# A table of steps in place of a list scheduler: attention block and gated MLP on one core

## The chip, the cores and the metric

The kernel runs on one core of a Trainium2 chip. The metric is the device time of one execution in microseconds (us). The engines are named as the profile names them: PE (TensorE, matrix products), DVE (VectorE), ACT (ScalarE), POOL (GpSimd) and SP (SyncE, which here only issues transfers). Each engine works through its own list of instructions. Transfers are carried by 16 DMA engines.

## The reference

A transformer block on 2048 tokens of width 512, in float32:

```python
qkv = (layernorm(x) @ wqkv).reshape(1, 2048, 3, 32, 16)      # 32 heads of 16
scores = einsum("bhqd,bhkd->bhqk", q, k) * 16 ** -0.5
scores = where((i - j >= 0) & (i - j < 256), scores, -1e9)   # a window of 256 keys
h = x + (softmax(scores) @ v) @ wo
n = layernorm(h)
out = h + (sigmoid(n @ w_gate) * (n @ w_up)) @ w_down         # hidden width 1376
```

## The kernel before

**Arithmetic.** float32 operands of the large products are split into a high and a low float16 part (`split`: `copy` makes the high part at L237 on ACT or L239 on DVE, `subtract` the low part at L244), and a product is three float16 products (`mm3`, L284: high x high, high x low, low x high). Weights get a power-of-two scale from their largest absolute value: `bound` (L249, L251) and `scale`, whose small product on PE is L262.

**Attention** goes by 8 blocks `b` of 256 tokens and, in a block, by 8 groups `g` of four heads. The pieces of work are generator functions. `do_ln` normalizes a tile of 128 tokens (statistics L417 on DVE, a power L423 on POOL, the scaling L432, the split) and turns it over on PE (L454) or by a DMA. `do_qk` makes queries and keys of a block, `do_v` the values (both in `mm3`), `do_keys` writes the keys to DRAM (L515) and loads them stacked three high into SK (L522), `do_queries` stacks the queries into SQ (L531). `do_s` computes the scores once for their row maxima: eight products (L585) into a ring of three PSUM banks, and after each one a row maximum on DVE (`row_max`, L570), which frees the bank. `do_m` turns the maxima into two extra rows of SQ. `do_st` computes the scores transposed with the maximum taken off (L639 to L650, a ring of two banks), ACT takes the exponentials (`exps`, L615), POOL masks them (`far` L623, `dia` L628). `do_pv` is the weighted sum over the values (L676, float32), its result goes to `rh` (high part L237, low part L688), is turned over by a DMA (L699, tile RT) and added on POOL (`do_o`, L706). `do_wo` divides by the softmax sum (L718, L720), splits (`whl`), turns over by a DMA (tile oT) and multiplies with `wo`.

**MLP.** The hidden width is cut into 512, 512 and 352 columns. The first four token tiles go one by one: `do_early` computes their first 512 columns while attention still runs, with PSUM copied to SQ on DVE (L830), and `do_gu` the rest. The other twelve go in pairs by a Strassen-like scheme, seven products in place of eight: `do_pair` prepares the sums of token halves, `do_T` the sums of weight quarters (load, split L904 and L906, four subtractions in the load's tile at L919, split again L923 on ACT and L926 on DVE), and `do_group` is one pair with one part of the hidden width: seven products of six matmuls each (L1027) in three PSUM banks, with evacuations and sums on ACT, DVE and POOL between them. `do_down` multiplies with `w_down` and stores.

**What sets the order.** The kernel is written for engines whose lists are fixed when it is built. Each generator yields, step by step, a cost for every engine that may do the step, the keys of what it needs, and the rings (PSUM banks, buffers) of which it takes a place. `Planner` runs a list scheduler over these: it keeps a clock for each engine, models the start of each ready step (`start`), and on each engine grants the ready step that starts first; among those within a small tolerance (`eps`) the one with the lowest priority number (`pick`). For a step that several engines may do it compares the modelled ends (`better`). All priorities, offsets and biases are numbers in one dictionary `C`, and `alt` leaves a step to one engine unless its name is in `C["alts"]`. PE's cost is stretched by a model of its clock (`stream`).

Of the kernel before, what the change touches and what calls it, by code (L numbers as in the profile page):

```python
# [36 lines left out]
T = 2048  # L37
# [21 lines left out]
C = dict(T=[148.182, 280.933], ln7=-7.501, s=5.429, pv=39.123, o=4.672, wo=[30.36, 31.212], v=[12.599, 24.978], qk=[-12.405, 3.564], ln=[-8.702, -6.351], m=-21.936, am=338.233, amd=118.201, sp=[287.055, -17.738], l2=[68.786, 20.751], ngu=4, gu=[64.904, 0.734], sd=[-171.116, 73.748], Tg=[16.516, 52.23], Tu=[-222.738, 17.484], Tb=[-146.461, -3.199], stash=155.192, l2b=-109.019, eps=0.064, prep=[-243.079, 245.157, 1.957, -60.084], alts=['hi', 'raw', 'whi', 'wsc', 'amax', 'pt', 'on', 'hhi', 'qk'], look=0.0, blog=413.973, bias={'ACT': -9.573, 'DVE': 7.071, 'POOL': -15.707}, pet=8, npv=2, down=6.634, lw=[-75.362, -59.481, -0.005, 74.029], lx=[-8.688, -47.634, 14.356, 9.926, 203.463, 96.796, 168.915], fill=[-71.831, 121.643, 130.507], clear=[-64.533, -23.452], write=-298.105, slack=167.929, stack=-112.133, off={'ln': [-166.66, -0.25, -4.616, -3.823, 11.91, 32.661, 62.31, 64.356], 'qk': [-171.929, -6.135, -32.431, 64.031, 63.96, -1.291, 0.767, 60.185], 'v': [188.33, 69.219, 54.263, -107.364, 206.961, 55.229, 34.243, 107.232], 's': [-163.512, -0.768, 31.21, 39.136, -344.985, -8.781, 4.748, 80.39], 'wo': [52.242, 40.433, 173.071, 59.896, 100.92, 72.757, 141.062, -184.237], 'o': [95.122, -281.215, 28.752, -120.215, 253.442, -30.242, -120.978, 95.302], 'pv': [-429.156, -31.744, 41.816, -12.207, -99.804, -46.682, 68.082, -169.17], 'm': [-74.099, -46.67, -98.34, -10.409, -56.92, 36.197, -114.381, -34.099]}, prep2=[89.331, -93.273, 2.384, 49.139], warm=[6.577, 9.585, 8.612, 11.534, 12.673, 21.472, 19.465, 25.332, 31.19])  # L59


LAG = {"PE": 0.2, "DVE": 0.2, "ACT": 0.19, "POOL": 0.1, "DMA": 0.0}
OWN = {"PE": 0.0, "DVE": 0.06, "ACT": 0.05, "POOL": 0.0, "DMA": 0.0}
TICK = 10.24 / 3
SWITCH = 0.095


class Planner:

# [7 lines left out]
    def __init__(self, rings):  # L77
        self.clock = dict.fromkeys(ENGINES, 0.0)
        self.clock[DMA_] = 0.65
        self.clock[POOL_] = 3.4  # L80
        self.moved = 0.0
        self.rings = rings
        self.freed = {r: [] for r in rings}
        self.done = {}
        self.parked = {}
        self.live = {e: [] for e in ENGINES}
        self.best = {}
        self.count = 0
        self.busy = {}
        self.on = None  # L90
        self.mode = 0

    def add(self, prio, piece, step=0.0):
        self.count += 1
        self.submit([prio, self.count, step, piece, next(piece), None])

    def submit(self, item):
        costs, needs = item[4][:2]
        for k in needs:
            if not isinstance(k[0], float) and k not in self.done:  # L100
                self.parked.setdefault(k, []).append(item)
                return
        times = [k if isinstance(k[0], float) else self.done[k] for k in needs]
        item[5] = {e: max([0.0] + [t + (OWN if f == e else LAG)[f] for t, f in times]) for e in costs}
        for e in costs:
            self.live[e].append(item)
            self.changed(e)

    def changed(self, eng):
        for e in (eng,) if eng in (PE_, DMA_) else (DVE_, ACT_, POOL_):  # L110
            self.best.pop(e, None)

    def mark(self, key, t):
        self.done[key] = t
        for item in self.parked.pop(key, ()):
            self.submit(item)

    def free(self, ring, n, t):
        self.freed[ring][n] = t
        self.best.clear()  # L120

    def start(self, eng, item):
        t = max(item[5][eng], self.clock[eng])
        rings = item[4][2] if len(item[4]) > 2 else ()
        for i, r in enumerate(rings):
            n = len(self.freed[r]) - self.rings[r] + rings[:i].count(r)
            if n >= 0:
                f = self.freed[r][n]
                if f is None:
                    return None  # L130
                t = max(t, f[0] + (OWN if f[1] == eng else LAG)[f[1]])
        return t

    def better(self, eng, t, item):

        costs = item[4][0]
        for e, cost in costs.items():
            if e != eng:
                first = sum(i[4][0][e] for i in self.live[e] if i[5][e] <= t + C["look"] and i[0] < item[0])
                if max(item[5][e], self.clock[e] + C["blog"] * first) + cost + C["bias"][e] < t + costs[eng] + C["bias"][eng]:  # L140
                    return True
        return False

    def pick(self, eng):
        if eng not in self.best:
            c = []
            for item in self.live[eng]:
                t = self.start(eng, item)
                if t is not None and not (len(item[4][0]) > 1 and self.better(eng, t, item)):
                    c.append((t, item[0], item[1], item))  # L150
            if c:
                t0 = min(c)[0] + C["eps"]
                c = min((x for x in c if x[0] <= t0), key=lambda x: x[1:3])
            self.best[eng] = c
        return self.best[eng]

    def grant(self, eng, t, item):
        costs = item[4][0]
        for e in costs:
            self.live[e].remove(item)  # L160
            self.changed(e)
        places = []
        for r in item[4][2] if len(item[4]) > 2 else ():
            places.append(len(self.freed[r]))
            self.freed[r].append(None)
            if r == "F":
                self.best.clear()
        self.on = eng
        more = item[4][3] if len(item[4]) > 3 else 1.0
        if eng == PE_ and len(item[4]) > 4 and costs[eng]:  # L170

            t += SWITCH * (self.mode != item[4][4])
            self.mode = item[4][4]
        elif eng == PE_ and costs[eng]:
            t += SWITCH * (self.mode != 0)
            self.mode = 0
        self.clock[eng] = end = self.stream(t, costs[eng], more) if eng == PE_ else t + costs[eng]
        if eng == DMA_:
            self.moved = max(t + 1.27 + max(0.0, costs[eng] - 1.295), self.moved) + more
            end = self.moved + (0.4 if costs[eng] > 1.2 else 0.95)  # L180
            self.clock[eng] = max(self.clock[eng], self.moved - 4.0)
# [1224 lines left out]
```

## Time and profile before

| | |
|---|---|
| median of 3 runs | 806.79 us (806.51 to 807.27) |
| profiled execution | 808.32 us, of it 806.3 us from the first to the last instruction |
| PE busy | 756.5 us, 94%, 6714 matmuls |
| DVE, ACT, POOL busy | 566.7, 449.2 and 379.0 us |
| mean granted PE clock | 0.987 |
| DMA | 95.68 MB moved, mean 119 GB/s |

Busy time is the union of an engine's instructions. Matmuls are pipelined and their ends are modelled, so of PE the idle time says more than the busy time. Attention fills the trace up to about 466 us, the first four tiles of the MLP lie up to about 560 us, and the pairs with the down products after that. In a list of waits a row names the instruction that waited and the one that released it, then the total in us, the number of waits and the longest. In the chain of waits and in a timeline a row begins with its start and its duration in us.

### The profile page before, as it was taken

The page shows a single profiled execution, that of the slowest core. Times are in us where ns is not written, and L with a number is a line of the kernel's source. Part 1 is how long each engine was busy: PE and PEld are TensorE (multiplying, and loading weights), DVE is VectorE, ACT ScalarE, POOL GpSimd, SP SyncE. Part 2 cuts the span into 40 slices and gives each one's busy share as a digit, 9 for nine tenths or more (in the row PEclk, how much of TensorE's full clock was granted, in tenths as well). Part 3 has the DMA queues.
Part 4 walks back from the last instruction along what each step waited for, and adds up shares of the span by engine and source line. Part 5 has one row for each costly group of instructions (what it writes and reads, how often), then busy time and mean ns, then how long its engine had stood idle before and what let it go on. Part 6 is the DMA issues. An engine that isn't in the chain of part 4 may idle for free.

```text
span 806.3 us, 18187 instructions
## 1 busy us (share of the span) xinstructions
PE 756.5 (94%) x6714; PEld 470.9 (58%) x6714; DVE 566.7 (70%) x1688; ACT 449.2 (56%) x767; POOL 379.0 (47%) x477
## 2 busy tenths in 40 slices
PE   5788989999999999999998779989999999999998
PEld 5565767666787668787675434445454545454443
DVE  6847999998989678488777959784372737364442
ACT  7833678776686577777676855551332323242321
POOL 9932355664454365545456875572533324141110
PEclk9899999999999999999999999999999999999999
DMA  9574565667573945433435635538243635342322
GB/s 335 187 178 146 125 104 108 147 128 167 99 176 103 150 76 101 128 101 108 93 77 152 149 84 159 165 84 164 59 110 75 112 80 105 75 102 50 72 42 69
DMA packets 168568, 95.68 MB, mean 119 GB/s; under 512 B 140640, under 2 KB 146784, under 8 KB 168480
## 3 DMA queue, kind: packets, MB, share of 16 engines
q1 hardware_dynamic: 168480, 94.54, 51.0%
q8 instruction: 52, 0.85, 0.4%
q14 instruction: 36, 0.29, 0.1%
HBM read 35.26 MB, written 13.11 MB: 60 GB/s over the span
## 4 chain that ended last, share of the span: by engine, by line
PE 65%; POOL 10%; DVE 7%; DMA 7%; issue 6%; ACT 4%; SPq 1%; DVEq 0%; POOLq 0%; ACTq 0%
PE mmp L284 25%; PE sp L1027 9%; PE pvp L676 7%; PE stp L1027 6%; PE sp L585 6%; PE pvp L1027 3%; PE stp L650 2%; PE stp L640 2%; DMA oT<-whl 2%; DMA xT<-hl 2%; ACT pa L615 2%; PE stp L639 1%; DVE junk L570 1%; PE stp L641 1%; DMA SK<-mem 1%
## 5 line engine op out<-in xcount | busy, mean ns | idle before, releaser
L570 DVE CUSTOM_DVE_ANT_0 junk<-sp,mask 128x320 bf16<-128x320 f32 (+4 forms) x512 | 209.6, 465 | 27.8 <-PE sp L585 27.1
L615 ACT ACTIVATE pa<-stp,kappa 128x512 f32<-128x512 f32 (+1 forms) x256 | 154.4, 645 | 17.3 <-PE stp L641 12.7
L585 PE MATMUL sp<-SK,SQ 96*128 96x256 f16 (+1 forms) x960 | 123.2, 232 | 5.7 <-DVE mq L570 2.4
L1027 PEld LDWEIGHTS <-SQ 128*128 128x128 f16 x756 | 73.9, 98 | 75.0
L284 PE MATMUL mmp<-xT,W 128*128 128x256 f16 x768 | 110.7, 275 | 1.8 <-ACT xT L237 0.8
L623 POOL TENSOR_SCALAR_AFFINE_SELECT pa<-pa 128x1024 f32<-128x1024 f32 x56 | 62.3, 1112 | 89.6 <-ACT pa L615 89.4
L284 PE MATMUL mmp<-WD,hT 128*128 128x512 f16 (+1 forms) x408 | 95.8, 379 | 1.3 <-DMA hT<-X 1.2
L585 PEld LDWEIGHTS <-SQ 96*128 96x128 f16 x960 | 78.1, 97 | 26.9 <-issue 14.8
L615 ACT ACTIVATE pb<-stp,kappa 128x512 f32<-128x512 f32 x128 | 83.2, 685 | 13.9 <-PE stp L650 12.5
L284 PEld LDWEIGHTS <-W 128*128 128x128 f16 x768 | 70.4, 98 | 11.2 <-issue 1.8
L284 PEld LDWEIGHTS <-hT 128*128 128x128 f16 (+1 forms) x408 | 39.6, 98 | 48.4 <-DMA hT<-X 2.9
L676 PE MATMUL pvp<-pa,VT 128*17 128x128 f32 (+1 forms) x1408 | 62.7, 307 | 0.4 <-POOL pa L628 0.2
L640 PE MATMUL stp<-SQ,SK 100*128 100x256 f16 x224 | 59.9, 272 | 0.0
L641 PE MATMUL stp<-SQ,SK 100*128 100x128 f16 x256 | 55.5, 219 | 1.8 <-DMA SQ<-mt 0.7
L284 PE MATMUL mmp<-WO,oT 128*128 128x512 f16 x192 | 53.1, 394 | 3.5 <-DMA oT<-whl 3.5
L639 PE MATMUL stp<-SQ,SK 100*128 100x128 f16 x224 | 49.4, 221 | 6.4 <-ACT pa L615 4.3
L284 PE MATMUL mmp<-W,xT 128*128 128x512 f16 x192 | 49.9, 386 | 5.2 <-POOL W L244 2.8
L628 POOL TENSOR_SCALAR_AFFINE_SELECT pa<-pa 128x512 f32<-128x512 f32 x64 | 43.0, 672 | 19.6 <-ACT pa L615 19.5
L676 PEld LDWEIGHTS pvp<-pa,VT 128*17 128x17 f32 x1408 | 37.5, 97 | 23.9 <-issue 1.9
L284 PEld LDWEIGHTS <-x 128*128 128x128 f16 x288 | 28.4, 99 | 37.5 <-issue 11.6
L628 POOL TENSOR_SCALAR_AFFINE_SELECT pb<-pb 128x512 f32<-128x512 f32 x64 | 41.8, 654 | 16.1 <-ACT pb L615 15.9
L650 PE MATMUL stp<-SQ,SK 100*128 100x256 f16 x256 | 46.3, 274 | 2.2 <-ACT pa L615 2.1
(281 smaller groups left out, 1388.0 us busy)
## 6 DMA issues: line engine op xcount, KB each, us to landing
SQ<-sq SPq DMA_DIRECT2D x96, 128.0 KB
SK<-mem SPq DMA_DIRECT2D x16, 384.0 KB
chunk<-in_wd_dram SPq DMA_DIRECT2D x20, 256.0 KB
mem<-sk SPq DMA_DIRECT2D x8, 512.0 KB
out_dram<-WO SPq DMA_DIRECT2D x16, 256.0 KB
X<-in_x_dram SPq DMA_DIRECT2D x7, 512.0 KB
chunk<-in_wu_dram SPq DMA_DIRECT2D x12, 256.0 KB
xs<-X SPq DMA_DIRECT2D x10, 256.0 KB
```

Of the source, the lines that this page charges most:

```text
L284: PE.matmul(ps, a_of(a, k), b_of(b, k), start=(k == 0 and i == 0), stop=(k == n - 1 and i == 2))
L570: V.tensor_tensor_reduce(out=junk[:, c0:], in0=ps[:, c0:], in1=mask[:, c0:], scale=1.0, scalar=-3.0e38, op0=ALU.add, op1=ALU.max, accum_ou ...
L585: PE.matmul(ps[:, col:col + k1 - k0], q, SK[0:96, (2 * a + hf) % 5, 4 * (p % 2) + j, k0:k1], start=True, stop=True)
L615: S.activation(dst, a, AF.Exp, scale=kappa)
L623: G.affine_select(out=f, in_=f, pattern=[[0, 8], [-1, 128]], compare_op=ALU.is_gt, fill=0.0, base=0, channel_multiplier=1)
L628: G.affine_select(out=p, in_=p, pattern=[[0, 4], [1, 128]], compare_op=ALU.is_ge, fill=0.0, base=0, channel_multiplier=-1)
L639: PE.matmul(a[:, 0:128], ks(k0, g, j), qs(b, g, j, 0, 128), start=True, stop=True)
L640: PE.matmul(a[:, 128:384], ks(k0 + 1, g, j), qs(b, g, j, 0, 256), start=True, stop=True)
L641: PE.matmul(a[:, 384:512], ks(k0 + 3, g, j), qs(b, g, j, 128, 256), start=True, stop=True)
L650: PE.matmul(a[:, u, :], ks(k0 + 2, g, j + u), qs(b, g, j + u, 0, 256), start=True, stop=True)
L676: PE.matmul(ps[32 * j:32 * j + 17, u, q0:q1], VT[:, kt % 6, 8 * j + g, :], w[:, j, c:c + q1 - q0], start=first, stop=last, skip_group_chec ...
L1027: PE.matmul(out, x7[p][0][:, kk, MATS[a], ha, :], mv, start=first and i == 0, stop=i == 5, skip_group_check=True)
```

## The change

`Planner` with its clocks, costs, priorities and the dictionary `C` goes. In its place a text, `TABLE`, names the steps in the order in which they are to be issued: `s0` is the next step of the first score piece, `s0.3` the fourth row maximum that it has spawned, `prep2/a*2` two steps of the third weight's preparation on ACT (`/v` is DVE, `/g` POOL). Pieces of one kind are numbered in the order in which they are added. `Order` keeps the same generators, checks that what a step needs has been issued and that its ring has a place, and sends it on. The costs that the generators yield now only list the engines that may do a step. All alternatives of `alt` are open, so steps change their engine too: by the table, DVE does 1102 steps where the planner gave it 1058, ACT 696 in place of 736, POOL 366 in place of 370; PE's 1766 and the 415 DMA steps are the same set in another order. The tests that asked whether several pieces were done become a counter (`join`), and `do_down` also needs both last `wo` tiles. Tiles, buffers, rings and matmuls are the same. The table was made by moving single steps and judging the result in replays with random delays.

```diff
-C = dict(T=[148.182, 280.933], ln7=-7.501, s=5.429, pv=39.123, ...
+NGU = 4
+PET = 8
+TABLE = """
+load_x0 load_x1 load_w1 load_w2 load_w0 load_w4 load_w3 fill1 zeros1 ln0 load_w5 load_w7 load_x3 load_w6 load_x2 load_w8 ln1 load_w9 load_w10 load_w15
...
+down14*2 down15*3
+"""
-class Planner:
+class Order:
     def __init__(self, rings):
...
-    def add(self, prio, piece, step=0.0):
-        self.count += 1
-        self.submit([prio, self.count, step, piece, next(piece), None])
+    def add(self, piece):
+        kind = (self.name + ".") if self.name else piece.__name__.replace("do_", "")
+        n = self.count[kind] = self.count.get(kind, -1) + 1
+        self.live[kind + str(n)] = [piece, next(piece)]
...
+    def join(self, key, n, t, last):
+        self.joins[key] = self.joins.get(key, 0) + 1
+        if self.joins[key] == n:
+            last(t)
...
-    def start(self, eng, item):
-    def better(self, eng, t, item):
-    def pick(self, eng):
-    def grant(self, eng, t, item):
-    def stream(self, t, cost, share):
...
+    def step(self, name, choice):
+        piece, (costs, needs, *rest) = self.live[name]
+        assert all(isinstance(k[0], float) or k in self.done for k in needs), name
         places = []
+        for r in rest[0] if rest else ():
+            n = len(self.freed[r]) - self.rings[r]
+            assert n < 0 or self.freed[r][n], (name, r)
             places.append(len(self.freed[r]))
             self.freed[r].append(None)
+        self.on = {"v": DVE_, "a": ACT_, "g": POOL_}[choice] if choice else next(iter(costs))
+        assert self.on in costs and (choice or len(costs) == 1), name
+        self.name = name
+        try:
+            self.live[name][1] = piece.send(((0.0, self.on), *places))
+        except StopIteration:
+            del self.live[name]
+
+    def run(self, table):
+        for token in table.split():
+            token, _, n = token.partition("*")
+            for _ in range(int(n or 1)):
+                self.step(*token.partition("/")[::2])
...
     def alt(name, own, **costs):
-        return costs if name in C["alts"] else {own: costs[own]}
+        return costs
...
-            e, *place = yield {PE_: 0.645}, [("h", t, f // 4), ("W", "d", f, 3)], [] if ps else ["mm"]
+            e, *place = yield {PE_: 0.645}, [("h", t, f // 4), ("W", "d", f, 3), ("wo", 14), ("wo", 15)], [] if ps else ["mm"]
...
-        plan.run()
+        plan.run(TABLE)
```

Two places at which the order differs follow. Line numbers of the new kernel are higher (L244 becomes L315, L351 L422, L919 L975, L688 L751, L830 L890, L706 L769).

The first is on POOL early on, before the first scores. `W1_90<-wv_112` is the low part of one quarter of the value weights, which `do_v` needs; `WO_78<-OS_80` is the same for `wo`, which is not needed before the first `do_wo`; `rs` and `nb` belong to a normalization, `SK_84` and `SQ0_77` memsets fill constant rows. Before:

```order
L244 TENSOR_TENSOR WO_78<-OS_80,WO_78 128x512
L423 TENSOR_TENSOR rs_486<-rs_486,nhalf_120 128x1
L425 TENSOR_SCALAR nb_584<-mv_484,rs_486 128x1
L423 TENSOR_TENSOR rs_506<-rs_506,nhalf_120 128x1
L425 TENSOR_SCALAR nb_592<-mv_504,rs_506 128x1
L244 TENSOR_TENSOR WO_78<-OS_80,WO_78 128x512
L244 TENSOR_TENSOR W1_90<-wv_112,W1_90 128x512
L244 TENSOR_TENSOR WO_78<-OS_80,WO_78 128x512
L244 TENSOR_TENSOR W1_90<-wv_112,W1_90 128x512
L423 TENSOR_TENSOR rs_524<-rs_524,nhalf_120 128x1
L425 TENSOR_SCALAR nb_629<-mv_522,rs_524 128x1
L244 TENSOR_TENSOR W1_90<-wv_112,W1_90 128x512
```

One quarter of the value weights stands just ahead of these rows, the other three are spread among `wo` and normalizations. The same place on POOL in the changed kernel:

```order
L315 TENSOR_TENSOR hl_347<-xn_306,hl_347 128x512
L494 TENSOR_TENSOR rs_323<-rs_323,nhalf_120 128x1
L496 TENSOR_SCALAR nb_388<-mv_321,rs_323 128x1
L422 MEMSET SQ0_77 4x1024
L422 MEMSET SK_84 4x1024 x2
L315 TENSOR_TENSOR W1_90<-wv_112,W1_90 128x512 x2
L315 TENSOR_TENSOR WO_78<-OS_80,WO_78 128x512
L315 TENSOR_TENSOR W1_90<-wv_112,W1_90 128x512 x2
L315 TENSOR_TENSOR WO_78<-OS_80,WO_78 128x512
L829 MEMSET amg_628 128x16
```

All four quarters now stand together with one quarter of `wo` between them; the other three quarters of `wo` and three normalizations have moved behind them.

The second place is the end of attention. On POOL `pa_8149` and `pb_8150` are the exponentials of the last group, `OS_80<-RT_79` is the add of `do_o`, and the `X_73<-X_73` row of eight is the subtractions of two pieces of `do_T` (the third and fourth). Before:

```order
L623 AFFINE_SELECT pa_8149<-pa_8149 128x8x128
L628 AFFINE_SELECT pa_8149<-pa_8149 128x4x128
L628 AFFINE_SELECT pb_8150<-pb_8150 128x4x128
L706 TENSOR_TENSOR OS_80<-RT_79 128x2x8x17
L919 TENSOR_TENSOR X_73<-X_73 128x256 x8
L1257 MEMSET X_73 128x2x32
L706 TENSOR_TENSOR OS_80<-RT_79 128x2x8x17
```

In the changed kernel POOL keeps the fourth piece's subtractions there:

```order
L686 AFFINE_SELECT pa_8138<-pa_8138 128x8x128
L691 AFFINE_SELECT pb_8139<-pb_8139 128x4x128
L975 TENSOR_TENSOR X_73<-X_73 128x256 x4
L769 TENSOR_TENSOR OS_80<-RT_79 128x2x8x17
L1309 MEMSET X_73 128x2x32
L769 TENSOR_TENSOR OS_80<-RT_79 128x2x8x17
```

and the third piece's four stand on DVE, ahead of the copy of the last but one weighted sum (`rh_8163`):

```order
L965 SCALAR_TENSOR_TENSOR Wg_7734<-X_73,sg_5896,Wg_7734 128x2x256 x2
L310 CAST X_73<-X_73 128x512
L975 TENSOR_TENSOR X_73<-X_73 128x256 x4
L751 SCALAR_TENSOR_TENSOR rh_8163<-pvp0_94,rh_8163 128x2x256
L965 SCALAR_TENSOR_TENSOR Wg_7734<-X_73,sg_5896,Wg_7734 128x2x256
L315 TENSOR_TENSOR X_73<-X_73 128x512
```

So of eight subtractions in a row on POOL four have gone to DVE and stand earlier in the program; nothing else was put in their place.

More of the change, by code (lines that the diff above doesn't have):

```diff
@@ L62 @@
[L62 to L65, printed above, removed]
-class Planner:
+NGU = 4
+PET = 8
+TABLE = """
+load_x0 load_x1 load_w1 load_w2 load_w0 load_w4 load_w3 fill1 zeros1 ln0 load_w5 load_w7 load_x3 load_w6 load_x2 load_w8 ln1 load_w9 load_w10 load_w15
+load_w11 load_w12 load_w14 load_w13 load_x7 load_x6 ln0 ln1 ln0/a*2 prep0/a prep0/v*2 ln1/v prep0/a ln1/a ln0/g fill1*2 ln1/g prep0*2 ln0 prep1/v prep0 ln0/v
@@ L134, in better @@
-    def better(self, eng, t, item):
[L136 to L142, printed above, removed]
-    def pick(self, eng):
[L145 to L155, printed above, removed]
@@ L164, in grant @@
             places.append(len(self.freed[r]))
             self.freed[r].append(None)
[L166 to L181, printed above, removed]
-        return ((end, eng), *places)
-    def stream(self, t, cost, share):
-        while cost > 1e-9:
-            n = int(t / TICK + 1e-9)
-            slow = 1 if self.busy.get(n - 1, 0.0) >= 0.385 * TICK else 2
-            d = min(cost * slow, (n + 1) * TICK - t)
-            self.busy[n] = self.busy.get(n, 0.0) + d / slow * share
-            cost -= d / slow
-            t += d
-        return t
@@ L258, in scale @@
     def scale(nm, amax, t):
[L260 removed]
+        t, n = yield {PE_: 0.22}, [t], ["s"]
         pt = psum_tile("s", [P, 512])
@@ L434, in layernorm @@
         plan.free(rings[0], nx, e)
-        return (yield from transposed(hl, rings[1], n, dst, [e] + after, list(more), key[0] == "x" and t < C["pet"]))
+        return (yield from transposed(hl, rings[1], n, dst, [e] + after, list(more), key[0] == "x" and t < PET))
     def split(src, pool, ring, e):
@@ L478, in do_ln @@
         plan.mark(("xT", b, i), e)
-        if all(("xT", 1, j) in plan.done for j in range(2)) and "hlw" not in plan.done:
-            plan.mark("hlw", e)
+        if b == 1:
+            plan.join("hlw", 2, e, lambda t: plan.mark("hlw", t))
     def do_qk(b, c, jj):
@@ L533, in do_queries @@
         plan.mark(("queries", b, p), e)
-        if all(("queries", b, i) in plan.done for i in range(4)):
-            plan.mark(("copied", b, 0), e)
+        plan.join(("copied", b), 4, e, lambda t: plan.mark(("copied", b, 0), t))
     def do_v(b, i):
@@ L826, in do_early @@
                 plan.mark(("gu", t, 0), e)
-                if all(("gu", t, i) in plan.done for i in range(3)):
-                    plan.free("x2", x2[t][1], e)
+                plan.join(("x2", t), 3, e, lambda z: plan.free("x2", x2[t][1], z))
             kept.append(H8[:, 2 * t + u].rearrange("p a t -> p (a t)").bitcast(F32))
@@ L836, in do_gu @@
         plan.mark(("gu", t, c), eu)
-        if all(("gu", t, i) in plan.done for i in range(3)):
-            plan.free("x2", x2[t][1], eu)
+        plan.join(("x2", t), 3, eu, lambda z: plan.free("x2", x2[t][1], z))
         yield from gated(t, c, g, u, eg, eu, ng, nu)
@@ L910, in do_T @@
             else:
[L911 to L914 removed]
+                plan.join(("w", nm, kk, part), 2, m, lambda t: [plan.mark(("W", nm, k, part), t) for k in (kk, kk + 2)])
         a, b, c_, d = f[:, 0, 0], f[:, 0, 1], f[:, 1, 0], f[:, 1, 1]
```

366 lines of the change are left out of this document (224 added, 142 removed).

## The prediction

> **What bounds the kernel now.** I read the page's head first, then a table of stages, then who PE waits for, and last the chain of waits and the timeline at the two places where those point.
>
> ```profile
> span 806.3 us, 18187 instructions
> PE 756.5 (94%) x6714; PEld 470.9 (58%) x6714; DVE 566.7 (70%) x1688; ACT 449.2 (56%) x767; POOL 379.0 (47%) x477
> ```
>
> No matmul is added or removed (the table holds the same 1766 PE steps), so only the 806.3 - 756.5 = 49.8 us in which PE stands idle can be won, and what PE loses at a lowered clock. The table of stages (window, length, then busy us of PE, PEld, DVE, ACT, POOL, the granted clock, the DMA share) says where that lies:
>
> ```profile
> core 0: us, PE busy (x) PEld busy (x) DVE busy (x) ACT busy (x) POOL busy (x), PEclk, DMA share, GB/s
> 36.30:46.10 9.80, 5.98 (x24) 2.23 (x25) 5.56 (x7) 6.74 (x11) 9.45 (x12) 1.00 0.58 143
> 46.10:63.50 17.40, 15.82 (x120) 11.73 (x120) 6.51 (x10) 4.18 (x7) 0.69 (x2) 1.00 0.75 202
> 63.50:128.00 64.50, 60.09 (x636) 44.59 (x635) 60.54 (x295) 41.22 (x84) 26.79 (x40) 0.97 0.55 124
> 128.00:420.00 292.00, 285.25 (x3671) 212.12 (x3672) 240.88 (x913) 214.25 (x351) 153.92 (x195) 1.00 0.55 116
> 420.00:466.00 46.00, 38.09 (x411) 22.43 (x400) 37.36 (x72) 35.79 (x59) 33.30 (x40) 0.93 0.59 146
> 466.00:499.00 33.00, 27.82 (x170) 11.93 (x170) 25.41 (x33) 16.89 (x24) 25.15 (x27) 0.95 0.48 118
> 499.00:560.00 61.00, 56.63 (x288) 27.73 (x287) 44.66 (x68) 28.48 (x45) 31.26 (x37) 1.00 0.58 136
> 560.00:802.40 242.40, 242.40 (x1202) 117.22 (x1199) 117.98 (x220) 73.26 (x130) 64.22 (x78) 1.00 0.39 81
> ```
>
> The last row is the first thing to see: from 560 us to the last matmul PE is busy all 242.40 us. No order can shorten that; it can only open gaps. The idle time lies before it: 3.8 us in the first row, 4.4 in the third, 6.8 in the fourth (spread over 292 us), 7.9 and 5.2 in the two rows at the end of attention, 4.4 in the next. Who PE waits for, in total us, number and longest:
>
> ```profile
> PE stp L639 <- ACT pa L615: 4.3, 7, 2.6
> PE sp L284 <- DVE SQ L830: 4.2, 2, 2.3
> PE mmp L284 <- DMA oT<-whl: 3.5, 3, 1.3
> ...
> PE mmp L284 <- POOL W L244: 2.8, 3, 1.4
> PE sp L585 <- DVE mq L570: 2.4, 4, 1.4
> PE stp L650 <- ACT pa L615: 2.1, 6, 1.0
> ...
> PE sp L585 <- DMA SK<-mem: 1.6, 1, 1.6
> ```
>
> No waits are long; an order can still help at several places, and three of them can be followed.
>
> **The change part by part.**
>
> *The value weights on POOL (36.3 to 46.1 us).* The chain of waits runs there through POOL's low parts of weights, then PE, then the load of the keys:
>
> ```profile
> 38.11 1.12 POOL W L244
> 39.23 1.12 POOL WO L244
> ...
> 43.25 1.56 POOL W L244
> ...
> 57.14 6.34 DMA SK<-mem
> ```
>
> `do_v` multiplies a quarter of the value weights as it comes; the quarters are late because POOL takes `wo` and normalizations between them, and PE is busy for 5.98 of 9.80 us. What these pieces cost on POOL:
>
> ```profile
> L423 POOL TENSOR_TENSOR rs<-rs,nhalf 128x1 f32<-128x1 f32 x10 | 6.2, 616 | 0.2
> L244 POOL TENSOR_TENSOR W<-wv,W 128x512 f16<-128x512 f32 x4 | 5.7, 1424 | 0.0
> L244 POOL TENSOR_TENSOR WO<-OS,WO 128x512 f16<-128x512 f32 x4 | 4.6, 1156 | 0.1
> ...
> L425 POOL TENSOR_SCALAR nb<-mv,rs 128x1 f32<-128x1 f32 x10 | 4.3, 426 | 1.0
> ```
>
> Ahead of the last quarter the new order leaves out three quarters of `wo`, 3 x 1.16 = 3.5 us, and three normalizations, 3 x (0.62 + 0.43) = 3.1 us: 6.6 us earlier on POOL than the 43.25 + 1.56 = 44.8 us at which it ends now, so about 38.2. PE cannot use all of it, since its first value product has waited for something else:
>
> ```profile
> 36.29 0.81 PE L284 MATMUL mmp<-W,xT 128*128 128x512 f16 x3 [1.39 <-DVE sq L506]
> ```
>
> It starts at 36.3, held by a PSUM bank that DVE's copy of the queries frees, and that isn't moved. The stage's 24 matmuls take 24 x 0.20 = 4.8 us back to back (242.40 us for 1202 in the table's last row). So they end at 41.1 in place of 46.1, 5.0 earlier. The keys' products follow at once in both orders, and their load, which ends the stage with PE waiting 1.6 us, starts as much earlier; the DMA share of 0.58 and 0.75 in the two rows leaves room, though the queries' transfers stand ahead of it. I take **-4.5**. Bounds: -1 (the high parts from ACT, busy 6.74 of 9.80, come late, or the keys queue behind the queries), -6 (the wait for the keys goes too).
>
> *The first scores (63.5 to 128 us).* DVE is busy 60.54 of 64.5 us, more than PE. Between the row maxima of the first and the seventeenth group the table leaves DVE three scalings of a normalization and one scan of a weight chunk fewer (they go to ACT, busy 41.22). Each is a pass over 512 columns, priced by the scaling:
>
> ```profile
> L432 DVE TENSOR_SCALAR xn<-X,mv,rs 128x512 f32<-128x512 f32 x6 | 3.2, 542 | 0.0
> ```
>
> 4 x 0.54 = 2.2 us. I take **-2**, bounds -4 (PE's 4.4 idle) and +2 (ACT late instead).
>
> *Steady attention (128 to 420 us).* PE is idle for 6.8 of 292 us and the table moves about ten scans of weight chunks from DVE to ACT there and little else. **0**, bounds -5 (most of the idle time goes) and +5; the rival below says why it may lose.
>
> *The end of attention (420 to 499 us).* The timeline, all engines (start, duration, in brackets the idle time before and its releaser):
>
> ```profile
> 471.06 7.34 POOL L919 TENSOR_TENSOR X<-X 128x256 f32<-128x256 f32 x8
> 473.83 2.75 PE L284 MATMUL sp<-W0u,x 128*128 128x512 f16 x12
> 474.68 1.15 ACT L923 ACTIVATE Tg<-X,sg 128x1024 f16<-128x1024 f32 x1 [5.19 <-POOL X L919]
> 475.73 0.58 ACT L237 ACTIVATE rh<-pvp 128x512 f16<-128x512 f32 x1
> 475.86 1.96 DVE L926 SCALAR_TENSOR_TENSOR Tg<-X,sg,Tg 128x512 f16<-128x512 f32 x2 [4.21 <-ACT Tg L923]
> 476.42 0.81 PE L284 MATMUL sp<-Wg,x 128*128 128x512 f16 x3
> ...
> 478.34 0.68 DVE L830 COPY SQ<-sp 128x512 f32<-128x512 f32 x1
> ...
> 479.07 0.59 PE L284 MATMUL sp<-Wg,x 128*128 128x512 f16 x2 [1.84 <-DVE SQ L830]
> ```
>
> ACT waits 5.19 us for the third piece's subtractions; the copy of the last weighted sum stands behind it, though PE has gone on to other products (the row of 473.83). DVE waits 4.21 us for ACT with the PSUM copy L830 behind it, and PE waits for that. With the subtractions done earlier on DVE both waits lose their cause; next in line are the fourth piece's four, still on POOL, at 7.34 / 8 = 0.92 each behind the masks. PE's two waits for L830 are 4.2 us. Second, the table puts six products of `do_early` ahead of the last weighted sum, where before stood two: 4 x 0.65 = 2.6 us of work (four such lie between 473.83 and 476.42) goes into the gaps in which PE waits for exponentials (4.3 and 2.1 us above). For the waits on oT I count nothing. Sum 4.2 + 2.6, about **-7**; bounds 0 (the gaps reappear elsewhere) and -13 (all idle time of both rows).
>
> What four subtractions cost on DVE is in the trace already, for another piece, beside three of POOL's:
>
> ```profile
> 447.21 3.18 POOL L919 TENSOR_TENSOR X<-X 128x256 f32<-128x256 f32 x3 [0.68 <-POOL X L919]
> 449.40 3.27 DVE L919 TENSOR_TENSOR X<-X 128x256 f32<-128x256 f32 x4
> ```
>
> Alongside, POOL needs 1.06 us for one, against 0.92 above; so they slow each other, and what a full exclusion would cost is a rival below. One rule of the Trainium skill speaks for that rival ("SBUF — State Buffer", section "Who interferes with whom"): a DVE instruction with two SBUF inputs and a POOL instruction that reads SBUF exclude each other. The trace agrees with it in direction, not in size.
>
> *500 to 560 us:* the same steps, with down products as fillers: **-1**, bounds -4 and +3. *From 560 us:* **+0.5**, bounds 0 and +4. The order mixes two groups and two tiles' down products step by step. A group's seventh product needs a sum made after its fifth. In the tightest case one product stood between them, without a gap on PE; now there are at least two, and on the mean more, so the cover has grown. The last group product is followed by 21 down products where it was 14, which changes nothing.
>
> Sum: -4.5 - 2 + 0 - 7 - 1 + 0.5 = -14. The span becomes 792.3 and the profiled execution 808.3 - 14 = 794.3; the runs' median lies 1.5 below that execution (806.79), so **793**.
>
> **The rivals.**
>
> *ACT bounds the end of attention.* From 420 to 466 us ACT is busy 35.79 of 46 us, mostly exponentials, and PE stands idle 7.9 us behind it. If order cannot change that, the -7 falls to about 0: 793 + 7 = 800. Against it: PE's waits named after exponentials are 4.3 + 2.1 us, less than the idle time.
>
> *POOL and DVE exclude each other.* Then the four subtractions on DVE, 3.27 us, push POOL's masks back by that much, and the weighted sums of the last groups with them: 793 + 3.3 = 796. Against it: POOL's 3.18 for three in the row above is not a full stop.
>
> *Slower: rows taken out of turn.* In the table 34 of the 512 row maxima and 16 of the 384 exponentials stand in another order than PE fills their banks; before, none did. The bank filled first is then held for one more instruction, in a ring of three (two for exponentials). DVE's row maximum and ACT's exponential take:
>
> ```profile
> L570 DVE CUSTOM_DVE_ANT_0 junk<-sp,mask 128x320 bf16<-128x320 f32 (+2 forms) x126 | 44.1, 402 | 6.7 <-PE sp L585 6.5
> ```
>
> ```profile
> L615 ACT ACTIVATE pa<-stp,kappa 128x512 f32<-128x512 f32 (+1 forms) x256 | 154.4, 645 | 17.3 <-PE stp L641 12.7
> ```
>
> 34 x 0.40 = 13.6 us and 16 x 0.65 = 10.4, together 24 us if PE has nothing else to do. From 14 / 24, about 60% of it exposed, the change loses; at 80% it is +19 - 14 = +5, 812. Against it: PE waited for row maxima 2.4 us in all.
>
> *No change.* The early gain is eaten by the keys' load (6.34 us, behind the queries) and the late one comes back between 499 and 560 us, where PE is idle 4.4 us: 806 to 807.
>
> **How the numbers follow.** My forecast has 58%, ACT's bound 14%, exclusion 10%, no change 7%, slower 11%. About 0.2%, 1.6 us, is what a measurement of this kernel can tell from no change. Faster is then 58 + 14 + 10 = 82%, within 0.2% 7%, slower 11%. Adding the terms' bounds outright gives -32 and +13, but they won't all fall to one side; I take 780 (-27) as the low end and 807 as the high one, which takes in ACT's bound, exclusion and no change and leaves out the slower case and a little at the low end.
>
> **What would show it.** Right: the span to the first row maximum falls from 63.5 to about 59; POOL's four W rows end before 39; ACT's `rh` of the last sum follows PE within 2 us and L830 disappears from PE's waits; PE from the first group on stays busy throughout. Wrong: the first scores still start after 62, PE's waits for L570 grow from 2.4 to over 8 us, or idle time appears in the last 242 us.

## The result, and the profile after

The changed kernel takes 784.25 us (median of 4 runs, 782.64 to 784.81) against 806.65 us for the kernel before: a ratio of 0.9722 (95% interval 0.9702 to 0.9743), 22.4 us less. Forecast were 793 (780 to 807), faster with a chance of 82%. The direction and the range held; the gain is 1.6 times the sum of 14.

The head of the changed kernel's page:

```profile
span 783.1 us, 18088 instructions
PE 747.0 (95%) x6714; PEld 469.7 (60%) x6714; DVE 601.7 (77%) x1762; ACT 427.0 (55%) x742; POOL 356.9 (46%) x443
```

PE does the same 6714 matmuls. Its idle time went from 49.8 to 783.1 - 747.0 = 36.1 us, and its busy time from 756.5 to 747.0. The table of stages of the changed kernel (columns as in the prediction; the windows are laid where the same work stands):

```profile
0.00:36.30 36.30, 21.93 (x202) 19.92 (x203) 28.76 (x74) 25.73 (x53) 31.21 (x47) 0.95 0.88 276
36.30:46.10 9.80, 9.71 (x72) 6.33 (x70) 6.93 (x12) 6.18 (x11) 5.69 (x9) 1.00 0.80 217
46.10:57.90 11.80, 11.60 (x84) 7.87 (x82) 4.41 (x7) 4.23 (x11) 1.38 (x4) 1.00 0.81 255
57.90:122.20 64.30, 58.52 (x614) 43.55 (x613) 58.38 (x281) 44.13 (x90) 28.08 (x41) 0.95 0.54 115
122.20:408.00 285.80, 284.46 (x3722) 213.64 (x3719) 245.30 (x922) 221.98 (x371) 149.56 (x192) 1.00 0.55 120
408.00:453.50 45.50, 37.73 (x386) 21.78 (x379) 40.27 (x80) 33.48 (x54) 30.50 (x38) 0.92 0.57 140
453.50:476.50 23.00, 21.26 (x152) 10.02 (x150) 21.82 (x31) 13.67 (x21) 16.80 (x17) 1.00 0.64 150
476.50:536.80 60.30, 59.31 (x304) 29.37 (x303) 50.10 (x79) 26.87 (x41) 30.52 (x37) 1.00 0.64 141
536.80:779.20 242.40, 242.40 (x1202) 117.25 (x1199) 144.99 (x279) 50.77 (x95) 63.21 (x62) 1.00 0.40 83
```

The last row is the row of before to the hundredth: 242.40 us without a gap. The early gap (3.82 us in 36.3 to 46.1) is gone; in steady attention PE is idle 1.34 us in place of 6.75; at the end of attention 7.77 and 1.74 stand where 7.91 and 5.18 stood; in the stage after it 0.99 in place of 4.37. Two rows got worse: the first scores, 5.78 in place of 4.41, and the first 36.3 us, 14.37 in place of 36.30 - 24.33 = 11.97 (there PE now waits for the largest absolute value of a weight, the first row below). Who PE waits for:

```profile
PE sp L333 <- DVE am L464: 10.8, 2, 10.1
PE stp L702 <- ACT pb L680: 4.2, 4, 2.8
PE mmp L525 <- ACT WO L320: 2.1, 1, 2.1
PE stp L702 <- DMA SQ<-mt: 2.0, 1, 2.0
PE sp L651 <- DVE mq L638: 1.6, 5, 0.4
...
PE sp L355 <- DVE SQ L890: 0.6, 1, 0.6
...
PE mmp L355 <- DMA oT<-whl: 0.2, 1, 0.2
```

The wait for the PSUM copy (L830, now L890) fell from 4.2 to 0.6, that for oT from 3.5 to 0.2, that for row maxima from 2.4 to 1.6; that for POOL's low parts of the value weights (2.8) is no longer listed. To see where the 23.24 us between the two profiles arise, the table gives for every profile the start in us of five places in PE's list, found by counting matmuls along the table's steps: the first score product, the score products of the seventeenth group, the transposed scores of the sixtieth, the first `do_gu` product, and the end of the last product.

| kernel | first score | group 17 | group 60 | `do_gu` | last end |
|---|---|---|---|---|---|
| before | 63.53 | 128.36 | 433.17 | 498.78 | 802.51 |
| changed | 57.87 | 125.21 | 419.97 | 479.00 | 779.27 |
| e1 old order | 63.61 | 130.03 | 434.50 | 498.55 | 800.92 |
| e2 new up to first scores | 58.10 | 125.73 | 429.57 | 493.77 | 797.27 |
| e3 new up to group 60 | 58.12 | 125.23 | 420.86 | 495.06 | 798.09 |
| e4 new from group 60 | 62.65 | 127.38 | 431.98 | 498.32 | 798.22 |
| e5 new, clean cut | 58.31 | 125.29 | 423.53 | 489.86 | 791.82 |
| e6 old, clean cut, then new | 62.06 | 125.99 | 429.83 | 489.49 | 788.56 |
| e7 new order, old engines | 64.86 | 134.90 | 437.99 | 500.55 | 806.70 |
| e8 old order, new engines | 62.50 | 127.59 | 437.54 | 501.26 | 809.44 |
| e9 subtractions on POOL | 58.35 | 125.57 | 421.78 | 483.92 | 782.94 |
| e10 rows in turn | 57.95 | 125.16 | 419.56 | 477.45 | 776.89 |
| e11 value weights first | 61.60 | 127.45 | 430.90 | 496.11 | 799.56 |
| e12 scans back on DVE | 58.03 | 125.41 | 421.98 | 479.83 | 779.85 |

From the first two rows, stage by stage: -5.7 up to the first score, +2.5 to group 17, -10.0 to group 60, -6.6 to `do_gu`, -3.5 behind it. Profiles with the same order up to a place differ there by some microseconds (group 17 by the old order: 126.0 to 130.0), so a stage's difference below about 2 us means nothing by itself. The middle is far clear of that: from group 17 to group 60 the old order takes 303.5 to 304.8 us in before, e1, e2, e4 and e11, and the new one 294.8 to 296.2 in the changed kernel, e3 and e9.

### The profile page after: what moved, and what is told of

The parts are those of the page before. It is cut to its first block, busy times and chain, and to the rows that moved or that the text cites. A ratio compares the mean times of both kernels' runs of the same rounds, so it can differ in the third digit from the quotient of the medians.

```text
span 783.1 us, 18088 instructions
## 1 busy us (share of the span) xinstructions
PE 747.0 (95%) x6714; PEld 469.7 (60%) x6714; DVE 601.7 (77%) x1762; ACT 427.0 (55%) x742; POOL 356.9 (46%) x443
## 5 line engine op out<-in xcount | busy, mean ns | idle before, releaser
L638 DVE CUSTOM_DVE_ANT_0 junk<-sp,mask 128x320 bf16<-128x320 f32 (+4 forms) x512 | 214.4, 465 | 26.6 <-PE sp L651 23.8
L680 ACT ACTIVATE pa<-stp,kappa 128x512 f32<-128x512 f32 (+1 forms) x256 | 157.4, 646 | 36.8 <-PE stp L704 33.1
L651 PE MATMUL sp<-SK,SQ 96*128 96x256 f16 (+2 forms) x960 | 127.6, 233 | 2.8 <-DVE mq L638 1.6
L355 PE MATMUL mmp<-WD,hT 128*128 128x512 f16 (+1 forms) x408 | 98.4, 379 | 0.6 <-DMA hT<-X 0.6
L355 PEld LDWEIGHTS <-hT 128*128 128x128 f16 (+1 forms) x408 | 39.8, 98 | 46.1 <-DMA hT<-X 0.9
L739 PE MATMUL pvp<-pa,VT 128*17 128x128 f32 (+1 forms) x1408 | 64.7, 315 | 0.0
L355 PE MATMUL mmp<-WO,oT 128*128 128x512 f16 x192 | 50.5, 379 | 0.6 <-DVE rh L312 0.4
```

Source lines behind the costliest of these rows:

```text
L355: PE.matmul(ps, a_of(a, k), b_of(b, k), start=(k == 0 and i == 0), stop=(k == n - 1 and i == 2))
L638: V.tensor_tensor_reduce(out=junk[:, c0:], in0=ps[:, c0:], in1=mask[:, c0:], scale=1.0, scalar=-3.0e38, op0=ALU.add, op1=ALU.max, accum_ou ...
L651: PE.matmul(ps[:, col:col + k1 - k0], q, SK[0:96, (2 * a + hf) % 5, 4 * (p % 2) + j, k0:k1], start=True, stop=True)
L680: S.activation(dst, a, AF.Exp, scale=kappa)
L739: PE.matmul(ps[32 * j:32 * j + 17, u, q0:q1], VT[:, kt % 6, 8 * j + g, :], w[:, j, c:c + q1 - q0], start=first, stop=last, skip_group_chec ...
```

## The experiments

All run the new kernel's code with another table. Ratios are to the kernel before on the same chip, with a 95% interval.

**e1: the old order in the new form.** The new table is replaced by the old planner's own steps; on every engine the list of instructions is the old one, row for row.

> The new kernel's code with a table that lists the old kernel's own steps: on each of the five engines every instruction stands where it stood before. Theory (only the order and the choice of engines count, not the way they are written down): 806.7, within 1 us of before. Rival (something else in the diff acts, such as the extra condition on the down products): the time moves by more than 1.6 us, towards 784.

Measured: 807.29 us, ratio 1.0021 (0.9997 to 1.0045). The way in which an order is written down, and the extra condition in `do_down`, are worth nothing that this measurement shows; the gain is in the table.

**e2: the new table up to the first scores only.**

```diff
 ... keys0 keys1 amax7
-s0 s0 s0 ln4 s0.0 ln4/a s0 s0.1 ...
+fill0 ln6/g ln7/g prep3/a prep3/g ln8/g ln9/g fill2/g s0 amax5/v s0 s0 ...
```

> The new table's steps up to the first score product, then all the others in the old order. In the profile of the changed kernel the first score product starts at 57.87 us in place of 63.53. Theory (the early gain is kept, since PE sets the pace afterwards): 806.7 - 5.7 = 801.0, and the first score product near 57.9 us. Rival (attention is paced by DVE, which is busy 60.54 of its first 64.5 us, or by the loads, so an early start is waited away): 804 to 807, with the gap at the seventeenth group back under 2 us.

Measured: 804.41 us, ratio 0.9967 (0.9944 to 0.9991). The first score starts at 58.10 as expected, but the time is the rival's: it falls by about 2, not 5.7, and at group 17 the lead over the old order's four profiles (126.0 to 130.0, mean 127.9) is 2.2 us. The changed kernel loses the same there (57.87 to 125.21 is 67.3 us, and 67.6 in e2; before it was 64.8). So an earlier start is partly given back in the first scores, in either order. What takes it back was not tried.

**e3 and e4: the new table up to the sixtieth group, and from there on.** At this place nine steps of the one and six of the other could not be issued yet and were put off to where they could.

```diff
 ... st58.7/a st58.6/a pv28
-st59 st59 amax23 st59.0/a st59 ln20/v ...
+m15 wo12/v st58.4/g wo12/v amax23 st58.5/g ln20/v ...
```

> The new table's steps up to the transposed scores of the sixtieth of the 64 groups (which start at 419.97 us in the changed kernel and at 433.17 before), then the others in the old order. Theory (the three stages add up: 5.7 before the first scores, 7.5 up to here, 10.0 behind): 806.7 - 13.2 = 793.5. Rival (the gain of the middle stage is only work put off, which has to be done behind it): 797 to 801.

> The old order up to the transposed scores of the sixtieth group, and the new table's order from there on. Theory (the end of attention gives its 10.0 us alone): 806.7 - 10.0 = 796.7; my prediction had 7.5 for it, 799.2. Rival (the end gains only because more of the other work has been done earlier): 800 to 807, and together with the run before the two gains fall short of 22.4.

Measured: 803.07 us, 0.9954 (0.9930 to 0.9977), and 805.41, 0.9983 (0.9962 to 1.0004). Both lie nearer to the rival (e3 even above its 797 to 801): e3 reaches group 60 at 420.86, as the changed kernel does, and then needs 74.2 us to `do_gu` where before needed 65.6. Its timeline at the seam shows a part of it (in brackets the idle time before, and its releaser):

```profile
447.77 4.63 PE L386 MATMUL mmp<-WO,oT 128*128 128x512 f16 x12 [3.95 <-DMA oT<-whl]
...
452.44 0.75 DVE L836 SCALAR_TENSOR_TENSOR X<-mmp,co,X 128x512 f32<-128x512 f32 x1 [6.49 <-PE mmp L386]
...
452.72 1.84 ACT L711 ACTIVATE pa<-stp,kappa 128x512 f32<-128x512 f32 x3 [8.21 <-PE stp L735]
...
455.17 1.16 POOL L346 TENSOR_TENSOR X<-X 128x512 f16<-128x512 f32 x1 [8.72 <-ACT X L339]
```

PE's next twelve products are those of `do_wo`, whose operand is still under way; it waits 3.95 us and works 4.63. In that time no scores come, so ACT stands for 8.21 us; DVE, whose next instruction adds the result of these products, stands for 6.49, and POOL, which waits for ACT, for 8.72. So the cut was at fault, or the stages don't add up; the next two runs tell.

**e5 and e6: the same, cut where both tables have issued the same steps up to one** (at the transposed scores of the fifty-ninth group). Nothing had to be put off.

```diff
 ... st57.8/g o27/g st57.4/g
-wo13/v*4 st58 st58.3/a v15 v15/a open_x20 ...
+st58 st58.3/a m15 st58 wo12/v v15 st58.4/g ...
```

> As in the run with the new table up to the sixtieth group, but cut one group earlier (at the transposed scores of the fifty-ninth), where the two tables have issued the same steps up to one, so that no step has to be put off. In the profiles that place starts at 425.55 us before and at 413.02 in the changed kernel. Theory (the stages add up and the first cut lost its gain at the seam, where 9 steps were out of place): 806.5 - 12.5 = 794.0. Rival (the front only puts off work of ACT and DVE, which the old order of the end cannot take up): 800 to 804 again.

> The old order up to the same clean cut, the new table's from there on. Theory (the end gives its own part): 806.5 - 10 = 796.5, and with the run before the two make about 22.4. Rival (the end's order pays only behind the new front): 803 to 806.

Measured: 794.53 us, 0.9866 (0.9844 to 0.9889), and 796.13, 0.9889 (0.9857 to 0.9922); expected were 794.0 and 796.5. By ratio the two save 1.34% and 1.11%, together 2.45% of the 2.78%, and the intervals cover the rest. So the stages do add up, and e3 and e4 had lost at their seams: a few steps out of place cost most of what a stage had gained. With e2's 2 us for the start taken off, the stretch from the first scores to the fifty-ninth group is worth 8 to 9 us by itself (8 by the ratios, 9 by the medians): the part for which the prediction had -2 and 0.

**e7 and e8: order and engines taken apart.** 170 steps change their engine. e7 keeps the new order and gives them back their old engines, e8 keeps the old order and gives them the new ones; a piece of it:

```diff
-... split0/a ln23/v T2/v pv30/v ...
+... split0/a ln23/v T2/g pv30/v ...
```

> The new table's order, but each of the 170 steps that has changed its engine goes back to the engine that had it before. Theory (my prediction's terms: about 6 of the gain are engine choices, scalings and scans on ACT instead of DVE and four subtractions on DVE instead of POOL, the rest is order): 784.3 + 6 = 790. Rival A (order is nearly all): 784 to 787. Rival B (order and engines belong together, each step placed for the engine that it has): above 797.

> The old order of all steps, with the new table's engines for the 170 that differ. Theory: 806.5 - 6 = 800. Rival A (order is nearly all): 804 to 807. Rival B (they belong together): 807 or above, since a step on another engine then stands at a place chosen for the old one.

Measured: 812.74 us, 1.0072 (1.0047 to 1.0098), and 812.35, 1.0075 (1.0042 to 1.0108). Both are slower than before, as rival B had it: each half alone loses about 6 us where the two together gain 22. Of PE's waits in e7:

```profile
PE sp L682 <- DVE mq L669: 6.9, 9, 1.5
PE stp L733 <- ACT pb L711: 6.1, 4, 3.5
```

The waits for row maxima, 1.6 us in the changed kernel, are 6.9 with DVE's old work back in a list that was laid out without it. In e8 the wait for oT is 7.1 us in place of 3.5:

```profile
PE mmp L386 <- DMA oT<-whl: 7.1, 5, 2.0
```

From group 17 to group 60, where the two together save 10.0 us, e7 takes 303.1 us, hardly less than the old order, and e8 310.0. So my way of adding up, a pass moved to another engine here, a reordering there, each with a price of its own, is not how this change works as a whole. A step has a place for the engine that does it.

**e9: the third piece's subtractions back on POOL**, directly ahead of the fourth piece's, all else as changed. So the step changes its engine and its place.

```diff
-... st63.2/a pv30/a T3/v ln23/v T2/v pv30/v st63 ... split2/v ln23 st63.8 T3/g o30 ...
+... st63.2/a pv30/a T3/v ln23/v pv30/v st63 ... split2/v ln23 st63.8 T2/g T3/g o30 ...
```

> The changed kernel with one step put back: the third piece's four subtractions on POOL, directly ahead of the fourth piece's, as before. Theory (my prediction's term for the end of attention: ACT's conversion, then its copy of the last weighted sum and DVE's copy from PSUM stand behind them, and PE waits 4.2 us): 784.3 + 4 = 788, with the wait of PE on the PSUM copy back at about 4 us. Rival (POOL is idle for 15.0 of 45.5 us there, so it takes 4 x 0.92 = 3.7 us more without anybody waiting): 784 to 785.5.

Measured: 788.49 us, 0.9752 (0.9724 to 0.9780); e10 and e12, run beside it, took 783.49 and 785.06. The ratio's interval overlaps the changed kernel's, but the fastest of e9's six runs, 787.06, is slower than the slowest of those ten, 786.12, and from group 60 to `do_gu` e9 needs 62.1 us where the changed kernel, e10 and e12 need 57.9 to 59.0. The span is 786.8, 3.7 more than the changed kernel's. The timeline of e9 shows the chain of the prediction link by link:

```profile
457.69 8.11 POOL L1006 TENSOR_TENSOR X<-X 128x256 f32<-128x256 f32 x8
...
462.08 1.15 ACT L1010 ACTIVATE Tg<-X,sg 128x1024 f16<-128x1024 f32 x1 [4.76 <-POOL X L1006]
...
463.14 0.58 ACT L339 ACTIVATE rh<-pvp 128x512 f16<-128x512 f32 x1
463.26 1.95 DVE L1013 SCALAR_TENSOR_TENSOR Tg<-X,sg,Tg 128x512 f16<-128x512 f32 x2 [2.61 <-ACT Tg L1010]
...
468.67 1.28 DVE L921 COPY SQ<-sp 128x512 f32<-128x512 f32 x2
...
469.40 1.44 PE L386 MATMUL sp<-W0u,x 128*128 128x512 f16 x3 [4.22 <-DVE SQ L921]
```

and of the changed kernel at the same place:

```profile
456.46 1.15 ACT L979 ACTIVATE Tg<-X,sg 128x1024 f16<-128x1024 f32 x1
...
456.79 4.69 POOL L975 TENSOR_TENSOR X<-X 128x256 f32<-128x256 f32 x4
...
458.93 0.60 ACT L308 ACTIVATE rh<-pvp 128x512 f16<-128x512 f32 x1 [1.32 <-PE pvp L739]
...
465.32 1.28 DVE L890 COPY SQ<-sp 128x512 f32<-128x512 f32 x2
...
466.06 0.81 PE L355 MATMUL sp<-W0u,x 128*128 128x512 f16 x3 [0.63 <-DVE SQ L890]
```

With eight subtractions on POOL, ACT waits 4.76 us for the first four, the copy `rh` of the last sum comes at 463.14 in place of 458.93 (e9 is 1.8 us behind already at group 60), DVE waits 2.61, and PE 4.22 in place of 0.63. ACT's copy in the changed kernel waits for nothing but PE, 1.32 us. The rival (POOL has idle time, so it costs nothing) falls: POOL's idle time does not lie where ACT waits.

**e10: row maxima and exponentials in turn.**

```diff
-... s2.6/v s2.5/v ...
+... s2.5/v s2.6/v ...
```

> The changed kernel with all row maxima and all exponentials put into the order in which PE fills their banks (70 row maxima and 32 exponentials change places among themselves, every other step stays). Theory (the inversions cost nothing, PE waits 1.6 us for row maxima): 784.3 within 1.6. Rival A (my slower rival in a small size: a bank held for one more instruction is partly exposed): 781 or less. Rival B (they are placed so because another order would be late): 786 or more.

Measured: 783.49 us, 0.9691 (0.9663 to 0.9719). PE's wait for row maxima is 1.2 us in place of 1.6. The theory holds and rival B falls; whether undoing the inversions gains a little (rival A wanted 781) stays open, since the interval overlaps the changed kernel's. It is the fastest table measured here, but not shown to beat it.

**e11: the value weights first, in the old order.**

```diff
-... qk5 queries3 prep3/g ... prep2/v v2 prep3/a ... prep2/g ... ln8/g ... prep2/g queries6
+... qk5 queries3 ... prep2/v v2 ... prep2/g prep3/g prep3/a prep3/a prep3/g ... ln8/g queries6
```

> The old order with 13 steps moved: all four quarters of the value weights on POOL ahead of the four of the output weights and three normalizations, ACT's copies of the output weights behind them too. Theory (my prediction's first term): the value products end 4 to 5 us earlier, the first score product starts near 59 to 60 us in place of 63.5, and since a start that is 5.4 us earlier was worth 2 us in the second run, the time is 806.0 - 2 = 804. Rival (the quarters' high parts come late as well, from ACT and DVE): first score product at 62 or later, no change in time.

Measured: 805.77 us, 0.9981 (0.9958 to 1.0005). The first score starts at 61.60, between the two expectations. The timeline of e11 and then of the changed kernel, POOL's low parts:

```profile
36.47 3.84 POOL L346 TENSOR_TENSOR W<-wv,W 128x512 f16<-128x512 f32 x3 [3.97 <-DVE W L341]
...
37.87 5.37 PE L386 MATMUL mmp<-W,xT 128*128 128x512 f16 x21 [0.35 <-DVE sq L608]
```

```profile
30.67 1.16 POOL L315 TENSOR_TENSOR W<-wv,W 128x512 f16<-128x512 f32 x1 [0.20 <-ACT W L308]
33.94 1.32 POOL L315 TENSOR_TENSOR W<-wv,W 128x512 f16<-128x512 f32 x1 [2.10 <-DVE W L310]
...
36.75 2.28 POOL L315 TENSOR_TENSOR W<-wv,W 128x512 f16<-128x512 f32 x2 [0.37 <-ACT W L308]
```

In e11 POOL now waits 3.97 us itself, for a quarter's high part from DVE; in the changed kernel the high parts come earlier, and what brings them was not tried alone. POOL's order by itself is worth 1.9 of the 5.7 us at most: the four profiles with the old order have their first score at 62.06 to 63.61, so 61.60 is hardly clear of them, and by the end there is nothing that the measurement separates from zero.

**e12: the middle's twelve scans back on DVE.**

```diff
-... amax9/a ... amax11/a ... amax13/a ... amax31/a ...
+... amax9/v ... amax11/v ... amax13/v ... amax31/v ...
```

> The changed kernel with the 12 scans of weight chunks that ACT took over between the seventeenth and the fifty-ninth group put back on DVE, at the same places. Theory (the middle gains because DVE, with 245 of 286 us busy, is relieved ahead of row maxima, 12 x 0.62 = 7.4 us): 784.3 + 4 = 788 or more, PE's waits for row maxima up from 1.6 us. Rival (my prediction's reading: these scans hide, and the middle gains by order alone): 784 to 785.5.

Measured: 785.06 us, 0.9715 (0.9687 to 0.9742): no difference from the changed kernel that the measurement shows. Waits for row maxima rise only from 1.6 to 2.1 us, and the stretch from group 17 to group 60 from 294.8 to 296.6, where the old order takes 303.5 or more. The scans hide almost wholly; the middle's gain is not theirs.

## Why the prediction was right, and where not

*What bounds the kernel.* "Only the idle time can be won, and what PE loses at a lowered clock" was too narrow. Idle time fell by 13.7 us, and PE's busy time by 9.5 with the same matmuls; the clock's mean of 0.987 and 0.989 accounts for 0.002 x 806 = 1.6 of that. In steady attention one matmul takes 285.25 / 3671 = 77.7 ns before and 284.46 / 3722 = 76.4 now. This difference, 3700 x 1.3 ns = 4.8 us, lies in rows in which PE counts as busy. A short wait can hide there: score products are recorded with 0.19 to 0.28 us each, while their starts follow each other by 0.03 to 0.11, so a short hold-up leaves no idle time. The rest of the 9.5 us lies before the first scores (PE busy 46.1 us there, now 43.2) and between group 60 and `do_gu` (52.5, now 49.5); it is not split further.

*The value weights, -4.5.* Measured -5.7 at the first score, and POOL's four rows end at 36.75 + 2.28 = 39.0, against 38.2 worked out and 39 as the mark. The size was about right, the reason was at most a third of it: by e11 POOL's order alone gives 1.9 or less. That the term fitted is therefore in good part luck. High parts that come late, the case of the bound -1, are what e11 ran into (there from DVE); in the changed kernel they came earlier, too.

*The first scores, -2.* Measured +2.5 between the two profiles, and e2 shows the same giving back. The step that failed is the reading that fewer passes on DVE shorten the stage. From its early start the old order (e2) takes 67.6 us to group 17, the new one 67.0 to 67.3 in the changed kernel, e3, e5 and e9, so the fewer passes are worth next to nothing. PE's longest wait there is now a transfer of the row maxima into SQ (2.0 us, in the list above; 0.7 before). That this is what takes the early start back is not shown.

*Steady attention, 0.* This is the term that was mis-sized: -10.0 to group 60, 8 to 9 us by e5 less e2, twice the lower bound of -5. I had counted which passes change their engine, found ten scans "and little else", and e12 confirms that these are worth next to nothing; but the order of the other steps I had costed at nothing as well. That was the step that failed.

The kept traces show which waits of PE went. Take, for each matmul from group 17 to group 60, the time since the start of the one ahead of it, less the median of that time for the same pair of products, and add up what exceeds 20 ns (the products of the weighted sums, 40.9 us in both kernels, left out). This counts hold-ups inside busy time, too. It gives 12.9 us before, 12.1 in e1 and 3.5 in the changed kernel; the drop of 9.4 is most of the 10.0. By what released PE it is 5.4 to 1.6 ahead of score products (DVE's row maxima, but for 0.2), 4.6 to 1.5 ahead of transposed scores (ACT's exponentials) and 2.5 to 0.4 ahead of `do_wo`'s products (the transfer into oT). So the gain has no single wait behind it.

Of the whole waits of PE and ACT in this stretch the views name, before (128 to 420 us) and changed (122.2 to 408):

```profile
PE mmp L284 <- DMA oT<-whl: 2.2, 2, 1.2
PE sp L585 <- DVE mq L570: 1.9, 2, 1.4
...
ACT rh L237 <- PE pvp L676: 36.9, 19, 4.3
ACT pb L615 <- PE stp L650: 9.5, 16, 2.5
ACT pa L615 <- PE stp L641: 8.6, 27, 0.6
```

```profile
PE sp L651 <- DVE mq L638: 0.7, 2, 0.4
PE mmp L355 <- DMA oT<-whl: 0.2, 1, 0.2
...
ACT pa L680 <- PE stp L704: 22.9, 44, 2.3
ACT rh L308 <- PE pvp L739: 19.9, 14, 2.3
ACT pb L680 <- PE stp L713: 10.7, 19, 1.8
```

Before, ACT reached its copy of a weighted sum 19 times ahead of PE and stood 36.9 us in all, with the next exponentials queued behind; now 14 times and 19.9 us. Its waits for scores rose in turn, from 18.1 to 33.6, so ACT waits for PE as long as before (55.0 and 53.5), but for scores, with no copy that stands in front. The better places of these copies can account at most for what PE lost to exponentials, 3.1 of the 10 us, and that they do is argued, not shown. By e7 the order without its engines saves at most 1.7 us in this stretch and by e8 the engines without the order lose 5. The scans are not the engine choice that matters; which one does was not tried.

*The end of attention, -7.* Measured -6.6. The part for L830, 4.2, is shown by e9 (3.7 us of span), where the waits come back in the order in which the prediction had them. The part for the early products, 2.6, was not tried alone; in the windows the first row kept its idle time (7.91 and 7.77) and the second lost 3.4.

*500 to 560 us, -1, and the rest, +0.5.* The idle time of the first of these stages went almost wholly (4.37 to 0.99, -3.4), within the bound of -4; the rest kept its 242.40.

*The rivals.* ACT's bound: half true, since the 7.9 us of idle time in the window of the last groups stayed. Exclusion of POOL and DVE: it is there, but it falls on the other side. The third piece's four subtractions, which moved to DVE, are the row of 452.73 below; the row of 435.76 is the second piece's, which DVE does in both kernels.

```profile
435.76 3.38 DVE L975 TENSOR_TENSOR X<-X 128x256 f32<-128x256 f32 x4
436.82 1.27 POOL L686 TENSOR_SCALAR_AFFINE_SELECT pa<-pa 128x1024 f32<-128x1024 f32 x1
...
439.17 1.15 ACT L979 ACTIVATE Tg<-X,sg 128x1024 f16<-128x1024 f32 x1 [2.75 <-DVE X L975]
...
440.95 0.22 PE L702 MATMUL stp<-SQ,SK 100*128 100x128 f16 x1 [2.80 <-ACT pb L680]
...
452.73 2.10 DVE L975 TENSOR_TENSOR X<-X 128x256 f32<-128x256 f32 x4
...
454.51 1.27 POOL L686 TENSOR_SCALAR_AFFINE_SELECT pa<-pa 128x1024 f32<-128x1024 f32 x1
```

The first two of 452.73 run while POOL is idle and take 0.41 and 0.42 us each; beside POOL's masks one takes up to 1.20. The lists of all such instructions (least, median and most in ns) say the same:

```profile
L975 DVE TENSOR_TENSOR X<-X x8: 411/673/1196, 435.8 to 454.1; 128x256 f32<-128x256 f32 x8
...
L686 POOL TENSOR_SCALAR_AFFINE_SELECT pa<-pa x56: 1087/1093/1539, 118.8 to 454.5; 128x1024 f32<-128x1024 f32 x56
```

So a mask grows from 1.09 to 1.27 us, and the masks are not pushed back by 3.3 us as the rival had it; DVE stands instead. By the section "Who interferes with whom" of the Trainium skill's page "SBUF — State Buffer", one side would have to stop for the other's whole instruction. The trace agrees with that for DVE's side: the subtraction that takes 1.20 us ends 0.3 us after the mask beside it. The prediction's "in direction, not in size" compared with 0.92 us for a subtraction on POOL, which is a mean over some beside DVE's work; the four that POOL begins at 472.31, with DVE idle, take 3.02 us together.

A chain like the third piece's still stands at the second one: ACT's conversion waits 2.75 us for DVE's subtractions, exponentials stand behind it, and PE waits 2.80 us for them, its longest wait at the end of attention. Before, its longest wait for exponentials, 2.6 us, ended a chain of this kind, too. What an order without it would give was not tried.

Rows out of turn: falls, by e10 and by the 1.6 us. No change: falls.

*The signs.* Of those for "right", the first score at 57.87 and ACT's `rh` close behind PE came true; POOL's four rows end at the mark of 39, not before it; L830's successor L890 is still among PE's waits with 0.6, and PE does not stay busy from the first group on (5.78 and 7.77 us idle in two rows). None of those for "wrong" appeared.

So the forecast was right in its sign and its range, and in the mechanism of one large term, the end of attention; the start fitted in size more than in its reason. The sum was 9.2 us short of the profile's 23.2: -2 and 0 were +2.5 and -10.0 (5.5 short), the stages from 500 us on gave 3.0 more and the start 1.2 more, and the end of attention 0.4 less (rounded).

## What to carry to other kernels

In this kernel, whose engines work through fixed lists, the order and the choice of engines belong together: taken over by halves, the change costs about 6 us, and a cut with nine steps out of place lost most of a stage's gain. Single moves can differ: twelve scans put back cost nothing that shows, four subtractions 3.7 us. So price a new order from each engine's waits, not from the passes that change engines, and look for the instruction that waits ahead of work that could run, as ACT's conversion did at the end of attention (e9). When two orders are to be compared by stages, cut where both have issued the same steps.

## What the runs showed that was not expected

One wait of PE of 3.95 us for an operand, with the 4.63 us of products behind it, left all other engines without work for 6.5 to 8.7 us (e3). An engine's idle share says little of its reserve: in the changed kernel POOL is idle 23.00 - 16.80 = 6.2 us between 453.5 and 476.5 us, and four subtractions more on it there (e9) still cost 3.7. And the busy time of PE in the profile changed by 9.5 us with the same matmuls, so busy time, as the profile counts it, is not a floor.
